# Placing the products of the spectral pairs further behind their elementwise pieces in a fused Fourier-mixer, ELU feed-forward and top-1 expert kernel

## Chip, cores and metric

The kernel runs on one core of a Trainium2 chip. The metric is the device time of one execution in microseconds (us), the median over runs.

## What is computed

Eight sequences of 3072 tokens with 256 channels pass through three layers:

```
X = rfft(x, axis=1);  Xr, Xi = X.real, X.imag
Yr = Xr @ w_r - Xi @ w_i + b_r
Yi = Xr @ w_i + Xi @ w_r + b_i
Y* = sign(Y*) * max(|Y*| - 0.01, 0)          # soft threshold, both parts
y  = irfft(Yr + 1j*Yi, n=3072)
h  = y @ w_in;  g = where(h > 0, h, exp(min(h, 0)) - 1)
z  = g @ w_out                               # feed-forward, d_ff 2048
# top-1 of 8 experts by normalised logits: out = gate * (relu(z @ w1[e]) @ w2[e])
```

Every product is done in three half-precision matmuls (high x high, high x low, low x high), so every operand is first split into a high half and a low half; these splits are the elementwise pieces named below.

## The kernel before

The program is a fixed order of instructions written out by hand: each engine runs its own list in order, and waits where an operand is not there. There are four stages. The first does the spectral layer of sequence 0. Then come eight batches, one for each sequence. A batch is 128 steps: 8 blocks of 384 tokens by 16 slices of the feed-forward layer. A step issues `ffn1` (six matmuls of 384 columns into a PSUM tile of `ps_h`, line 527, then exponential and relu on ScalarE, lines 539 and 540, and the maximum on VectorE, line 543) and `ffn2` of a slice four steps back (nine matmuls of 264 columns into `ps_a`, line 553). Every second step also splits two slices, high half on ScalarE (line 98, `copy_hi`) and low half on VectorE (line 101, `copy_lo`), into `ghl`. The last stage is the expert layer.

While batch b runs its feed-forward, the spectral layer of sequence b + 1 is threaded between the steps; the eighth batch has none. A list `plan` of (position in steps, function) says where. An entry at 53.3 is issued in step 53 between `ffn1` and `ffn2`, one at 53.6 after `ffn2`. Its parts, for each sequence:

- 16 `unit_a` (line 181, first transform), each after a `split_x` of its input; SyncE writes the results to DRAM (`b_d`, line 192), and `load_b` (line 200) reads them back as `b_in`, in another layout.
- 12 `pair`s, each of two groups of frequencies: a generator that `OFF` cuts into 17 pieces, placed at offsets from the pair's start. Starts run evenly from `PA` to `PZ`. Pieces 0 and 1 are the first product (line 222, from `b_in` into tile ps0) with the high split and a copy on ScalarE (lines 98, 234); 2 to 5 are elementwise on VectorE, VectorE, ScalarE, VectorE (lines 101, 242, 98, 101: `s_t`, `sm`); 6 is the first mixing product (line 210, from the `s_t` made of `sm`, with `k` on ScalarE, line 261, and `u` on GpSimd, line 262); 7 and 8 are the other mixing products; 9 to 12 are the threshold on VectorE (lines 276, 281, 290: `mt`, `mc`, `my`); 13 splits the high half `mm` on ScalarE (line 297), 14 the low half (line 299); 15 is the inverse product (line 304), with the high split of `do`; 16 its low split and the write to `e_d` (line 316).
- `unit_e` (line 329), two for each block, reads `e_d` back through `load_e` (line 204) and makes the next feed-forward input `yT`.

`ps_h` has four PSUM buffers, taken in turn: `ffn1`, `unit_a`, `unit_e`, the routing product (line 629) and the four products of a pair (pieces 0, 6, 7, 15) all draw from this ring in the stages after the first, so a tile must have been read by ScalarE and VectorE before the fourth product after it. The splitting of expert weights (GpSimd, lines 504 to 506) and its DMAs (`wl`, line 476 or 479; `wexp_d`, line 507) are issued at fixed steps, and so stand in SyncE's list between the others.

Of the kernel before, what the change touches and what calls it, by code (L numbers as in the profile page):

```python
# [15 lines left out]
ALU = mybir.AluOpType  # L16
# [3 lines left out]
B, S, D = 8, 3072, 256  # L20
# [19 lines left out]
XP = 2  # L40
JC = 4
CG, CN, CV = 4, 12, 8
PA, PZ = 44.0, 108.0
OFF = (0, 0.5, 1.0, 1.5, 2.0, 2.5, 3.5, 5.0, 5.5, 6.0, 6.5, 7.0, 7.5, 8.3, 8.8, 10.2, 11.0)
NP = NJ // 2
CD = (1, 2, 3, 5, 6, 7)
LAM = float(np.float32(0.01))
# [7 lines left out]
def kernel(  # L55
# [22 lines left out]
    act, dve, pool, pe, sp = nc.scalar, nc.vector, nc.gpsimd, nc.tensor, nc.sync  # L78
# [18 lines left out]
    def copy_hi(o, i, k):  # L97
        act.activation(out=o, in_=i, func=AF.Copy, scale=k)  # L98

    def copy_lo(o, i, k, hi):  # L100
        dve.scalar_tensor_tensor(out=o, in0=i, scalar=k, in1=hi, op0=ALU.mult, op1=ALU.subtract)  # L101
# [56 lines left out]
    def load_x(b, i):  # L158
        src = x[b].rearrange("(n m) c -> n m c", m=N2)[:, 4 * i : 4 * i + 4, :]
        if b == 0:  # L160
            if i == 0:
                xpc[0] = pre.tile([96, N2, D], F32, name="x_0")
            t = xpc[0][:, 4 * i : 4 * i + 4, :]
        else:
            t = xp.tile([N1, 4, D], F32, tag="xpc", name="xpc")
        sp.dma_start(out=t, in_=src)
        xpc[b, i] = t

    def split_x(b, g):
        src = xpc[b, g // 2][:, 2 * (g % 2) : 2 * (g % 2) + 2, :]  # L170
        t = xs.tile([N1, 2, 2, D], F16, tag="xsp", name="xsp")
        copy_hi(t[:, 0], src, 2.0**9)
        copy_lo(t[:, 1], src, 2.0**9, t[:, 0])
        xsp[b, g] = t
# [22 lines left out]
    def load_b(b, c):  # L197
        if c < NJ // JC:
            b_in[b, c] = bc.tile([128, JC, 2 * D], F16, tag="b_in", name="b_in")
            sp.dma_start(out=b_in[b, c], in_=b_d[b % 2][:, c * JC : (c + 1) * JC, :])  # L200

    def load_e(b, blk):
        e_in[b, blk] = ec.tile([96, 4, 2 * D], F16, tag="e_in", name="e_in")
        sp.dma_start(out=e_in[b, blk], in_=e_d[b % 2][:, 4 * blk : 4 * blk + 4, :])
# [10 lines left out]
    def pair(b, p):  # L215
# [27 lines left out]
        if p == 0:  # L243
# [3 lines left out]
                out=s2z[:, 0, :, 0:1], in0=z[:, :, 1:2], scalar1=2.0**-12, scalar2=None, op0=ALU.mult  # L247
# [11 lines left out]
        k = mx.tile([128, D], F32, tag="k1", name="k1")  # L259
# [3 lines left out]
            out=u, in0=bias[:, 0 if p else 1], in1=k[:, None, :].to_broadcast([128, 2, D]), op=ALU.add  # L263
# [6 lines left out]
        if p == 0:  # L270
# [3 lines left out]
        c = mx.tile([128, 2, D], F32, tag="mc", name="mc")  # L274
        y = mx.tile([128, 2, D], F32, tag="my", name="my", bufs=2)
        dve.scalar_tensor_tensor(
            out=t, in0=ps2.rearrange("p (r d) -> p r d", r=2), scalar=2.0**-10, in1=u, op0=ALU.mult, op1=ALU.add
# [7 lines left out]
        for jj in range(2):  # L285
            for r in range(2):
                i = slice(64 * jj, 64 * jj + 64)
# [3 lines left out]
                else:  # L291
                    dve.scalar_tensor_tensor(
                        out=o, in0=c[i, r, :], scalar=-1.0, in1=t[i, r, :], op0=ALU.mult, op1=ALU.max
                    )
            yield
        m = mx.tile([128, 2, 2, D], F16, tag="mm", name="mm", bufs=2)
        act.activation(out=m[:, 0], in_=y, func=AF.Copy)  # L297
        yield
        pool.tensor_tensor(out=m[:, 1], in0=y, in1=m[:, 0], op=ALU.subtract)  # L299
        yield  # L300
        ps3 = spec_ps()
        for jj in range(2):
# [14 lines left out]
            out=e_d[b % 2][8 * p : 8 * p + 8].rearrange("(j q) m x -> (q m) j x", j=2),  # L317
# [21 lines left out]
    def step_a(b, i):  # L339
        def one():  # L340
            if i + 2 < 16:
                split_x(b, i + 2)

        def two():
            if b and i % 2 == 1 and (i - 1) // 2 + XP < 8:
                load_x(b, (i - 1) // 2 + XP)
            unit_a(b, i)

        return one, two

    def units_e(b, blk):
        return [lambda cc=cc: unit_e(b, blk, cc) for cc in range(2)]
# [168 lines left out]
    def ffn1(b, blk, f, prev):  # L521
        y = yT[b, blk]
        ps = ps_h.tile([128, 512], F32, tag="h", name="ps_h")
        n = 0
        for cc in range(2):
            for i, h in ((0, 0), (0, 1), (1, 0)):
                pe.matmul(  # L527
                    ps[:, 0:BLK],
                    lhsT=win[:, i, cc, f * 128 : (f + 1) * 128],
                    rhs=y[:, h, cc, :],  # L530
                    start=n == 0,
                    stop=n == 5,
                )
                n += 1
        if f % 2 == 0:
            h_t[b, blk, f // 2] = tp.tile([128, 2, BLK], F32, tag="g", name="g")
        g = h_t[b, blk, f // 2][:, f % 2]
        e = tp.tile([128, BLK], F32, tag="e", name="e")
        act.activation(out=e, in_=ps[:, 0:BLK], func=AF.Exp, scale=2.0**-19)  # L539
        act.activation(out=e, in_=e, func=AF.Relu, scale=-(2.0**19), bias=top)  # L540
        if prev:
            split_hi(prev)
        dve.scalar_tensor_tensor(out=g, in0=e, scalar=-1.0, in1=ps[:, 0:BLK], op0=ALU.mult, op1=ALU.max)  # L543
        if prev:
            split_lo(prev)
# [125 lines left out]
    with tc.tile_pool(name="pre", bufs=1, side="right") as pre:  # L671
        for k in range(8):
# [5 lines left out]
                out=wm[ri].rearrange("p (k c) -> p k c", k=2), in_=w.rearrange("(k p) c -> p k c", p=128)  # L678
# [7 lines left out]
        for src, parts in (  # L686
# [3 lines left out]
            for lo, hi, v, r in parts:  # L690
                first.append(
                    lambda src=src, lo=lo, hi=hi, v=v, r=r: pool.dma_start(
                        out=bias[lo:hi, v, r, :], in_=src.partition_broadcast(hi - lo)
# [44 lines left out]
        for i in range(NP + 2):  # L738
# [3 lines left out]
            if i == 0:  # L742
                dve.tensor_scalar(
                    out=bias, in0=bias, scalar1=16.0, scalar2=-LAM * 16.0, op0=ALU.mult, op1=ALU.add
# [301 lines left out]
    NS = NBLK * NF  # L1046
    for b in range(B):
        plan = []
        for blk in range(1, NBLK):
            at = (2, 4, 9, 20, 30, 40, 50)[blk - 1] if b + 1 == B else 16 * blk - 11  # L1050
            if blk > 1:
                plan.append((max(0, at - 6), lambda blk=blk: load_e(b, blk)))
            for n, u in enumerate(units_e(b, blk)):
                plan.append((at + 1.5 * n, u))
        if b + 1 < B:
            plan.append((0, lambda: [load_x(b + 1, k) for k in range(XP)]))
            for i in range(2):
                plan.append((2.5 + i, lambda i=i: split_x(b + 1, i)))
            for i in range(16):
                for m, fn in enumerate(step_a(b + 1, i)):  # L1060
                    plan.append((3.4 + 2.25 * i + 0.6 * m, fn))
            for c in range(3):
                plan.append((41.2, lambda c=c: load_b(b + 1, c)))
            for k in range(NP):
                p = PA + (PZ - PA) * k / (NP - 1)
                gen = pair(b + 1, k)
                for o in OFF:
                    plan.append((p + o, lambda gen=gen: next(gen)))
                if k % 2 == 1 and k > 1:
                    plan.append((p + 0.2, lambda k=k: load_b(b + 1, k // 2 + 2)))  # L1070
            for blk in range(2):
                plan.append((NS - 6.2, lambda blk=blk: load_e(b + 1, blk)))
            for n, u in enumerate(units_e(b + 1, 0)):
                plan.append((NS - 2.6 + n, u))
        plan.sort(key=lambda p: p[0])
        if b + 1 == B:
            plan.append((60, open_moe))
        for blk in range(NBLK):
            for f in range(NF):
                step = blk * NF + f  # L1080
                ffn1(b, blk, f, pend.pop(0) if pend and f % 2 == 0 else None)
                if f % 2:
                    pend.append((b, blk, f // 2))
                while plan and plan[0][0] < step + 0.5:
                    plan.pop(0)[1]()
                run_late(1 + (len(late) > 1))
                todo.append((b, blk, f))
                lag = LAG + 1 if todo[0][2] == 0 or f == LAG + 1 else LAG
                while len(todo) > lag:
                    pop_ffn2()  # L1090
                while plan and plan[0][0] < step + 1:
                    plan.pop(0)[1]()
                run_late(1 + (len(late) > 1))
                c = b * NBLK + blk
                if f in wexp_at.get(c, ()):
                    if nw[0] + 1 < 8 * NE:
                        wexp_load(nw[0] + 1)
                    wexp_split(nw[0])
                    nw[0] += 1
        for _, u in plan:  # L1100
            u()
    while pend:
        k = pend.pop(0)
# [9 lines left out]
    for i in range(len(seq) + 1):  # L1113
# [12 lines left out]
        for h in range(2):  # L1126
            if 0 <= i - h < len(seq):
                kind, k = seq[i - h]
# [110 lines left out]
```

## Time and profile before

| what | value |
|---|---|
| median of 3 runs | 4063.5 us (4059.53 to 4069.39) |
| the profiled execution | 4070.74 us, of which span 4069.0 us |
| TensorE (PE) matmuls busy | 3719.3 us, 91% |
| VectorE (DVE) busy | 2586.8 us, 64% |
| ScalarE (ACT) busy | 2344.9 us, 58% |
| GpSimd (POOL) busy | 1428.6 us, 35% |
| mean granted TensorE clock | 0.967 of full speed |

The busy times are of one profiled execution on the chip, and times in the views count from the first instruction. A row names the line of the kernel, the engine, the operation and the tiles as out<-in. Idle time of an engine is put down to whatever ended it last. PEld is the loading of weights on TensorE, which overlaps matmuls. Because the matmuls are pipelined, the start of the next instruction tells the pace better than the duration of one.

### The profile page before, as it was taken

The page shows a single profiled execution, that of the slowest core. Times are in us where ns is not written, and L with a number is a line of the kernel's source. Part 1 is how long each engine was busy: PE and PEld are TensorE (multiplying, and loading weights), DVE is VectorE, ACT ScalarE, POOL GpSimd, SP SyncE. Part 2 cuts the span into 40 slices and gives each one's busy share as a digit, 9 for nine tenths or more (in the row PEclk, how much of TensorE's full clock was granted, in tenths as well). Part 3 has the DMA queues.
Part 4 walks back from the last instruction along what each step waited for, and adds up shares of the span by engine and source line. Part 5 has one row for each costly group of instructions (what it writes and reads, how often), then busy time and mean ns, then how long its engine had stood idle before and what let it go on. Part 6 is the DMA issues. An engine that isn't in the chain of part 4 may idle for free. (4 is left out here: it accounts for less than half of the span.)

```text
span 4069.0 us, 80617 instructions
## 1 busy us (share of the span) xinstructions
PE 3719.3 (91%) x31580; PEld 2909.5 (72%) x31580; DVE 2586.8 (64%) x5366; ACT 2344.9 (58%) x4738; POOL 1428.6 (35%) x1669
## 2 busy tenths in 40 slices
PE   5798898889889998988998898899999999999998
PEld 3566666667666666766666676667787899999998
DVE  7766676767666676766666776766565555555554
ACT  4676686668667666866776686667752222222221
POOL 3223323333333333333233323333234444344443
PEclk7899999999999999999999999999999999999999
DMA  6331132113112221211221131111035355534332
GB/s 191 99 85 49 45 97 61 54 48 106 46 46 79 73 62 48 88 53 56 63 86 51 44 99 60 54 53 56 20 101 128 78 154 152 147 79 113 95 82 78
DMA packets 290223, 323.25 MB, mean 79 GB/s; under 512 B 172197, under 2 KB 239023, under 8 KB 281520
## 3 DMA queue, kind: packets, MB, share of 16 engines
q1 hardware_dynamic: 238688, 197.12, 18.7%
q0 software_dynamic: 51152, 120.97, 8.9%
q8 instruction: 247, 4.05, 0.4%
q14 instruction: 136, 1.11, 0.1%
HBM read 335.96 MB, written 120.36 MB: 112 GB/s over the span
## 5 line engine op out<-in xcount | busy, mean ns | idle before, releaser
L553 PE MATMUL ps_a<-wout,ghl 128*128 128x264 f16 x9216 | 1229.9, 281 | 4.6 <-DVE ghl L101 3.7
L527 PE MATMUL ps_h<-yT,win 128*128 128x384 f16 x6144 | 1180.3, 330 | 15.9 <-DVE g L543 9.5
L543 DVE SCALAR_TENSOR_TENSOR g<-e,ps_h 128x384 f32<-128x384 f32 x1024 | 564.4, 551 | 802.4 <-ACT e L540 799.6
L553 PEld LDWEIGHTS <-ghl 128*128 128x128 f16 x9216 | 906.8, 100 | 223.0 <-DVE ghl L101 5.3
L527 PEld LDWEIGHTS <-win 128*128 128x128 f16 x6144 | 602.5, 99 | 340.3 <-issue 36.8
L539 ACT ACTIVATE e<-ps_h 128x384 f32<-128x384 f32 x1024 | 494.5, 483 | 440.6 <-PE ps_h L527 421.9
L968 ACT ACTIVATE r<-ps_h 128x512 f32<-128x512 f32 (+1 forms) x440 | 244.7, 556 | 803.9 <-PE ps_h L962 780.2
L540 ACT ACTIVATE e<-e,top 128x384 f32<-128x384 f32 x1024 | 629.9, 615 | 33.2
L962 PE MATMUL ps_h<-xt,wbuf 128*128 128x256 f16 (+1 forms) x5280 | 557.1, 263 | 6.5 <-DMA wbuf<-wexp_d,wix_f 6.5
L101 DVE SCALAR_TENSOR_TENSOR ghl<-g,ghl 128x768 f16<-128x768 f32 x512 | 506.3, 989 | 82.5 <-ACT ghl L98 79.4
L983 PE MATMUL ps_a<-wbuf,g 128*128 128x256 f16 x4776 | 554.6, 273 | 2.1 <-DVE g L970 1.1
L962 PEld LDWEIGHTS <-wbuf 128*128 128x128 f16 x5280 | 478.5, 98 | 56.9 <-DMA wbuf<-wexp_d,wix_f 6.8
L983 PEld LDWEIGHTS <-g 128*128 128x128 f16 x4776 | 465.0, 98 | 56.8 <-DVE g L970 2.2
L98 ACT ACTIVATE ghl<-g 128x768 f16<-128x768 f32 x512 | 423.4, 827 | 0.6 <-DVE g L543 0.6
L210 PE MATMUL ps_h<-wmix,s_t 128*128 128x256 f16 x1590 | 242.9, 284 | 178.7 <-DVE s_t L101 150.0
L1001 POOL DMA_INDIRECT out_dram<-o,mt x199 | 207.9, 1044 | 524.1 <-DVE o L993 301.3
L648 POOL DMA_INDIRECT rows_d<-row,pi x192 | 205.5, 1070 | 512.1 <-DMA rows_d<-row,pi 210.1
L969 DVE CAST g<-r 128x512 f16<-128x512 f32 (+1 forms) x440 | 177.6, 404 | 285.0 <-ACT r L968 282.6
L210 PEld LDWEIGHTS <-s_t 128*128 128x128 f16 x1728 | 164.2, 102 | 259.1 <-DVE s_t L101 182.8
L970 DVE TENSOR_TENSOR g<-r,g 128x512 f16<-128x512 f32 (+1 forms) x440 | 282.7, 643 | 15.1
L299 POOL TENSOR_TENSOR mm<-my,mm 128x512 f16<-128x512 f32 x96 | 125.3, 1305 | 462.3 <-ACT mm L297 461.8
L593 POOL TENSOR_TENSOR row<-xf,row 128x256 f16<-128x256 f32 x192 | 157.0, 818 | 297.5 <-ACT row L592 296.9
(191 smaller groups left out, 3547.5 us busy)
## 6 DMA issues: line engine op xcount, KB each, us to landing
b_d<-ao SPq DMA_DIRECT2D x128, 192.0 KB, 2.2
b_in<-b_d SPq DMA_DIRECT2D x48, 512.0 KB, 5.8
e_d<-do SPq DMA_DIRECT2D x96, 256.0 KB, 2.2
e_in<-e_d SPq DMA_DIRECT2D x64, 384.0 KB, 5.8
xpc<-in_x_dram SPq DMA_DIRECT2D x56, 384.0 KB, 4.1
wl<-in_moe_w_dram SPq DMA_DIRECT2D x64, 256.0 KB, 3.1
wexp_d<-wh SPq DMA_DIRECT2D x64, 256.0 KB, 3.5
raw<-in_moe_w_out_dram SPq DMA_DIRECT2D x8, 512.0 KB, 7.9
```

Of the source, the lines that this page charges most:

```text
L98: act.activation(out=o, in_=i, func=AF.Copy, scale=k)
L101: dve.scalar_tensor_tensor(out=o, in0=i, scalar=k, in1=hi, op0=ALU.mult, op1=ALU.subtract)
L210: pe.matmul(o, lhsT=st(h, cc), rhs=wmix[:, w, i, cc, :], start=first and n == 0, stop=last and n == 5)
L527: pe.matmul(ps[:, 0:BLK], lhsT=win[:, i, cc, f * 128 : (f + 1) * 128], rhs=y[:, h, cc, :], start=n == 0, stop=n == 5,)
L539: act.activation(out=e, in_=ps[:, 0:BLK], func=AF.Exp, scale=2.0**-19)
L540: act.activation(out=e, in_=e, func=AF.Relu, scale=-(2.0**19), bias=top)
L543: dve.scalar_tensor_tensor(out=g, in0=e, scalar=-1.0, in1=ps[:, 0:BLK], op0=ALU.mult, op1=ALU.max)
L553: pe.matmul(a_t[b, blk][t][:, 0:WOC], lhsT=g[:, h, f % 2, t * 128 : (t + 1) * 128], rhs=wout[:, f, i, :], start=f == 0 and n == 0, stop=f ...
L962: pe.matmul(ps[:, j, 0:n], lhsT=w[:, c : c + 128], rhs=xt[:, 2 * h + cc, :], start=m == 0, stop=m == 5)
L968: act.activation(out=r[:, :, 0:n], in_=ps[:, :, 0:n], func=AF.Relu, scale=2.0**-9)
L970: dve.tensor_tensor(out=g[:, q, 1, :, 0:n], in0=r[:, :, 0:n], in1=g[:, q, 0, :, 0:n], op=ALU.subtract)
L983: pe.matmul(ps[:, 0:D], lhsT=g[:, f // 2, h, f % 2, t * 128 : (t + 1) * 128], rhs=w[:, c : c + 256], start=m == 0, stop=m == 23,)
```

## The change

The offsets between pieces become longer. The first mixing product (piece 6) moves from 3.5 to 4.8 steps, so from 1.0 to 2.3 steps behind the last piece it reads (piece 5, at 2.5); the other mixing products from 5.0 and 5.5 to 7.0 and 7.5; the threshold follows; the inverse product (piece 15) moves from 10.2 to 14.2, so from 1.4 to 3.7 steps behind the low split of `mm`. Pairs start at 41.0 to 102.8 in place of 44.0 to 108.0, one every 5.62 steps in place of 5.82. The low split of `mm` goes from GpSimd to VectorE in all but the first sequence. The first transforms stand 2.1 steps apart in place of 2.25, the first two loads of x for a sequence are issued 8 steps before the end of the batch ahead, and the loads of `b_in` are placed at 38.8 in place of 41.2.

```diff
-PA, PZ = 44.0, 108.0
-OFF = (0, 0.5, 1.0, 1.5, 2.0, 2.5, 3.5, 5.0, 5.5, 6.0, 6.5, 7.0, 7.5, 8.3, 8.8, 10.2, 11.0)
+PA, PZ = 41.0, 102.8
+OFF = (0, 0.5, 1.0, 1.5, 2.0, 2.5, 4.8, 7.0, 7.5, 8.0, 8.5, 9.0, 9.5, 10.0, 10.5, 14.2, 15.2)
...
-        pool.tensor_tensor(out=m[:, 1], in0=y, in1=m[:, 0], op=ALU.subtract)
+        (dve if b else pool).tensor_tensor(out=m[:, 1], in0=y, in1=m[:, 0], op=ALU.subtract)
...
-            plan.append((0, lambda: [load_x(b + 1, k) for k in range(XP)]))
+            if b == 0:
+                plan.append((0, lambda: [load_x(b + 1, k) for k in range(XP)]))
+            if b + 2 < B:
+                plan.append((NS - 8, lambda: [load_x(b + 2, k) for k in range(XP)]))
             for i in range(2):
-                plan.append((2.5 + i, lambda i=i: split_x(b + 1, i)))
+                plan.append((2.5 + i if b == 0 else 0.5 + 1.2 * i, lambda i=i: split_x(b + 1, i)))
             for i in range(16):
                 for m, fn in enumerate(step_a(b + 1, i)):
-                    plan.append((3.4 + 2.25 * i + 0.6 * m, fn))
+                    plan.append((4.4 + 2.1 * i + 0.6 * m, fn))
             for c in range(3):
-                plan.append((41.2, lambda c=c: load_b(b + 1, c)))
+                plan.append((38.8, lambda c=c: load_b(b + 1, c)))
```

VectorE's list for the third pair of the sequence handled in the fourth batch (`s_t<-ps_h` is piece 2, `sm` piece 3, `s_t<-sm` piece 5, `my` pieces 11 and 12 of the pair before), first as it was:

```order
L101 SCALAR_TENSOR_TENSOR s_t<-ps_h,s_t 128x2x256
L290 TENSOR_TENSOR my<-mt,mc 64x256 x2
L604 TENSOR_REDUCE mxv<-lg 128x3
L543 SCALAR_TENSOR_TENSOR g<-e,ps_h 128x384
L242 TENSOR_TENSOR sm<-ps_h,sm 128x256
L290 TENSOR_TENSOR my<-mt,mc 64x256 x2
L606 TENSOR_TENSOR lg<-lg,mxv 128x24
L608 SCALAR_TENSOR_TENSOR eq<-lg,wdec 128x24
L543 SCALAR_TENSOR_TENSOR g<-e,ps_h 128x384
L101 SCALAR_TENSOR_TENSOR ghl<-g,ghl 128x768
L101 SCALAR_TENSOR_TENSOR s_t<-sm,s_t 128x2x128
```

And the same pair as it is now:

```order
L101 SCALAR_TENSOR_TENSOR s_t<-ps_h,s_t 128x2x256
L242 TENSOR_TENSOR sm<-ps_h,sm 128x256
L543 SCALAR_TENSOR_TENSOR g<-e,ps_h 128x384
L101 SCALAR_TENSOR_TENSOR ghl<-g,ghl 128x768
L101 SCALAR_TENSOR_TENSOR yT<-ps_h,yT 128x384
L276 SCALAR_TENSOR_TENSOR mt<-ps_h,u 128x512
L101 SCALAR_TENSOR_TENSOR s_t<-sm,s_t 128x2x128
```

The four `my` instructions of the pair before no longer stand between the pieces that the first mixing product waits for; one `mt` does. A little later in the same list stands the instruction that came from GpSimd (line 299):

```order
L543 SCALAR_TENSOR_TENSOR g<-e,ps_h 128x384
L101 SCALAR_TENSOR_TENSOR ghl<-g,ghl 128x768
L290 TENSOR_TENSOR my<-mt,mc 64x256 x2
L101 SCALAR_TENSOR_TENSOR do<-ps_h,do 128x2x256
L602 TENSOR_TENSOR lg<-xf,ss 128x24
L604 TENSOR_REDUCE mxv<-lg 128x3
L543 SCALAR_TENSOR_TENSOR g<-e,ps_h 128x384
L299 TENSOR_TENSOR mm<-my,mm 128x512
```

Four instructions stand between it and the last `my` that it reads. SyncE's list in the fourth batch around the first loads of `b_in`, as it was:

```order
L204 DMA e_in<-e_d 96x2048
L192 DMA b_d<-ao 96x2x512 x4
L476 DMA wl<-in_moe_w_dram 128x512
L507 DMA wexp_d<-wh 128x2x512
L200 DMA b_in<-b_d 128x2048 x3
L204 DMA e_in<-e_d 96x2048
```

And now:

```order
L204 DMA e_in<-e_d 96x2048
L192 DMA b_d<-ao 96x2x512 x3
L200 DMA b_in<-b_d 128x2048 x3
L476 DMA wl<-in_moe_w_dram 128x512
L507 DMA wexp_d<-wh 128x2x512
L204 DMA e_in<-e_d 96x2048
```

The three loads stood behind the write of `wexp_d`, which waits for GpSimd; they now stand right behind the last write of `b_d`.

## Rows read from the trace of the kernel before

**Rows 1.** Busy time by stage: seven batches with spectral work, the eighth batch, the experts.
```profile
core 0: us, PE busy (x) PEld busy (x) DVE busy (x) ACT busy (x) POOL busy (x), PEclk, DMA share, GB/s
...
172.00:2727.00 2555.00, 2307.67 (x18650) 1702.71 (x18648) 1722.22 (x3560) 1801.50 (x3685) 835.95 (x1045) 0.97 0.22 64
2727.00:2999.00 272.00, 265.94 (x2169) 196.63 (x2167) 167.72 (x383) 210.58 (x423) 93.57 (x138) 1.00 0.22 64
2999.00:4069.00 1070.00, 1050.52 (x10096) 944.76 (x10093) 568.55 (x1164) 248.17 (x452) 447.05 (x432) 0.99 0.41 107
```

**Rows 2.** Waits of PE from 172 to 2727 us: us in total, times, longest.
```profile
PE ps_h L210 <- DVE s_t L101: 145.3, 70, 4.8
PE ps_h L304 <- POOL mm L299: 30.5, 14, 3.2
PE ps_h L210 <- ACT s_t L98: 19.1, 35, 0.9
PE ps_h L222 <- DMA b_in<-b_d: 11.7, 6, 2.7
PE ps_h L304 <- ACT mm L297: 9.4, 7, 1.3
PE ps_h L527 <- DVE g L543: 9.0, 14, 0.8
PE ps_h L329 <- DVE do L101: 4.9, 7, 0.7
PE ps_h L527 <- DVE do L101: 4.7, 7, 0.7
PE ps_h L210 <- DVE g L543: 4.6, 7, 0.7
```

**Rows 3.** Timeline of PE, fourth batch, second and third pair: start, length, count, idle before.
```profile
1391.47 0.39 PE L210 MATMUL ps_h<-wmix,s_t 128*128 128x256 f16 x2 [0.93 <-ACT s_t L98]
1394.99 1.03 PE L210 MATMUL ps_h<-wmix,s_t 128*128 128x256 f16 x4 [3.12 <-DVE s_t L101]
...
1409.51 1.14 PE L527 MATMUL ps_h<-yT,win 128*128 128x384 f16 x6
...
1411.50 1.14 PE L527 MATMUL ps_h<-yT,win 128*128 128x384 f16 x6
...
1419.69 1.03 PE L210 MATMUL ps_h<-wmix,s_t 128*128 128x256 f16 x4 [4.77 <-DVE s_t L101]
```

**Rows 4.** Timeline of DVE ahead of the last of these waits.
```profile
1412.18 0.84 DVE L290 TENSOR_TENSOR my<-mt,mc 64x256 f32<-64x256 f32 x2
...
1413.60 0.42 DVE L242 TENSOR_TENSOR sm<-ps_h,sm 128x256 f32<-128x256 f32 x1
...
1418.26 1.37 DVE L101 SCALAR_TENSOR_TENSOR s_t<-sm,s_t 128x256 f16<-128x256 f32 x1
```

**Rows 5.** Timeline of POOL at the same time.
```profile
1417.95 1.41 POOL L299 TENSOR_TENSOR mm<-my,mm 128x512 f16<-128x512 f32 x1 [10.09 <-ACT mm L297]
```

**Rows 6.** Tile s_t in the fourth batch: ns min/median/max.
```profile
L101 DVE SCALAR_TENSOR_TENSOR s_t<-sm,s_t x12: 412/418/1376, 1376.4 to 1585.7; 128x256 f16<-128x256 f32 x12
```

**Rows 7.** Tile g of the experts, 3200 to 3300 us: ns min/median/max.
```profile
L970 DVE TENSOR_TENSOR g<-r,g x43: 424/693/694, 3200.0 to 3300.0; 128x512 f16<-128x512 f32 x36, 128x256 f16<-128x256 f32 x7
```

**Rows 8.** Busy time in the fourth batch: stretch of first transforms, stretch of pairs (columns of rows 1).
```profile
1264.00:1366.00 102.00, 101.29 (x797) 73.45 (x795) 75.80 (x153) 86.93 (x180) 33.48 (x48) 1.00 0.31 91
1366.00:1610.00 244.00, 210.21 (x1712) 156.25 (x1710) 159.16 (x335) 157.32 (x325) 84.34 (x102) 0.95 0.15 49
```

**Rows 9.** Timeline of SP's DMA issues, fourth batch, before the first pair.
```profile
1340.55 15.28 SPq L192 DMA_DIRECT2D b_d<-ao  x4
...
1363.59 0.38 SPq L507 DMA_DIRECT2D wexp_d<-wh  x1
1364.14 1.93 SPq L200 DMA_DIRECT2D b_in<-b_d  x3
```

**Rows 10.** Timeline of PE: last first transform, first product of the first pair.
```profile
1352.31 0.81 PE L181 MATMUL ps_h<-xsp,f_sb 96*96 96x512 f16 x3
...
1368.78 0.51 PE L222 MATMUL ps_h<-t_sb,b_in 128*128 128x128 f16 x6 [1.23 <-DMA b_in<-b_d]
```

## The prediction

> **What bounds the kernel now.** I read the busy times by stage first. In the seven batches that carry spectral work, TensorE is busy 2307.7 of 2555 us at 0.97 of its full clock; in the eighth batch, which has the same feed-forward work and no pairs, it is busy 265.9 of 272 us at full clock [rows 1]. So TensorE sets the pace, and what it loses lies in the seven batches: 2555 - 2307.7 = 247.3 us idle, and 3% of 2555 = 77 us from granted clock at the lower of its two levels (1.2 for 2.4 GHz). Within one batch the loss is local. The stretch of first transforms loses 0.7 us and keeps the clock at 1.00; the stretch of pairs loses 244 - 210.2 = 33.8 us and has a clock of 0.95, so another 12 us [rows 8].
>
> The waits say for what [rows 2]. The first mixing product waits for `s_t`: 145.3 us for VectorE's half and 19.1 us for ScalarE's, 164.4 in all, about 2 us for each of 84 pairs. The inverse product waits 30.5 + 9.4 = 39.9 us for `mm`. The first product of a sequence waits 11.7 us for `b_in`. A third kind is waits of a product for a `ps_h` buffer that VectorE has not yet read: 9.0 + 4.9 + 4.7 + 4.6 = 23.2 us. The rest is under a us each or little more.
>
> Idle time and clock together are 324 us. The profiled execution took 4070.7 us, 7.2 us above the median of the runs. With none of the 324 us left it would take 3747 us. (Some us of the idle time fell in stretches at the low clock and stand in both terms, so this floor is rather low than high.)
>
> **The change part by part.**
>
> *First mixing product.* A plain step takes 1411.50 - 1409.51 = 1.99 us [rows 3], for 6 x 384 + 9 x 264 = 4680 columns, so six matmuls of 256 columns take 1.99 x 1536/4680 = 0.65 us. Piece 6 moves 1.3 steps further from the last piece that it reads: 2.6 us. For most pairs the inverse product of the pair two before (at 14.2 - 11.2 = 3.0 steps) now stands in that gap too: 3.2 us of cover. The average wait of 2 us is under this. The two large ones of a batch are not: the second pair waits 0.93 + 3.12 = 4.05 us and has no inverse product in its gap, so 4.05 - 2.6 = 1.45 remain; the third waits 4.77 us, so 1.57 remain [rows 3]. That is 3.0 us for each batch, 21 us for seven, of 164. Bounds: nothing remains, since the four `my` that stood in VectorE's list between `sm` and its predecessor are gone from there, and two of them took 0.84 us ahead of `sm` [rows 4]; or twice as much, 40 us, if routing work meets more pairs than these two at the new spacing. I take 21.
>
> *Inverse product.* 2.3 steps or 4.6 us of further distance, against a longest wait of 3.2 us [rows 2]: all 39.9 us go.
>
> *Low split on VectorE.* It adds an instruction of 512 elements in each of 84 pairs. VectorE's subtraction of the same shapes and types in the expert stage takes 693 ns [rows 7], so 8.3 us for each batch. The product that reads it stands 3.7 steps or 7.4 us behind, and it replaces an instruction of GpSimd that took twice as long (1.41 us [rows 5]). Queued behind it are VectorE's `g` and `ghl` of the next step, so the cost, if its cover is gone, is 0.69 us each time, 58 us in all. There is also a gain: VectorE's `s_t<-sm` took 1.37 us where its median is 0.42 [rows 4, 6], and it ended 0.27 us after the GpSimd split that ran beside it [rows 5]. Without that split such delays become rarer. I cost it at nothing, with 0 and 58 us as ends; the range keeps both.
>
> *Loads of b_in.* The last first transform starts at 1352.31, its write to `b_d` has been issued by 1355.8, and the loads are issued only at 1364.14, right behind the write of `wexp_d`; the product starts at 1368.78, 4.6 us after, and had waited 1.23 us [rows 9, 10]. Now nothing stands between the last write and the loads. If a write lands about as late as a load, 4.6 us, the data are there at the latest 9.2 us after the issue, so 12.7 us after the start of the transform. TensorE reached the product at 1368.78 - 1.23, which is 15.2 us after the transform; the distance shrinks by two steps (37.75 to 44 becomes 36.5 to 41, counted by the places that steps offer), so to 11.3 us. A write is a small transfer and should land well before 4.6 us, so I take 0 of the 11.7 us as left; the upper end is 1.4 us for each batch, 10 us.
>
> *The ring of ps_h.* This is what is late next. The products of the pairs are now spread (offsets 0, 4.8, 1.4 and 3.0 within a spacing of 5.62, where they stood at 0, 3.5, 5.0 and 4.4 within 5.82), which favours it. But TensorE no longer pauses, so ScalarE and VectorE no longer catch up in the pauses. In the stretch of pairs VectorE is busy 159.2 + 8.3 = 167.5 us and ScalarE 157.3, against 210 - 12 = 198 us of TensorE at full clock: 85% and 79% [rows 8]. ScalarE ran at 86.9/102 = 85% in the stretch of first transforms, and TensorE lost 0.7 us there [rows 8]; a share of 85% alone does not stop it. I take the ring's 23 us times 1.5: 35 us, with 10 and 70 as ends. The closer first transforms (2.1 steps) are in this term.
>
> *Clock.* At both stretches where TensorE idles little the clock is 1.00 [rows 1, 8]. With the waits of 4 us gone I take 10 of 77 us as left; ends 0 and 25.
>
> *Loads of x.* Two loads move from the start of a batch to eight steps before it, onto SyncE's list, and nothing on TensorE waited for x in rows 2. No cost, and no gain.
>
> Sum: 3747 + 21 + 35 + 10 = 3813 us against 4070.7, and 7 less against the median: **3806 us**.
>
> **The rivals.**
>
> *Half comes back.* The elementwise chain itself may be too slow: ScalarE waits for VectorE and VectorE for ScalarE within a pair, and at 85% in-order lists leave little room, so the waits move to the feed-forward's own `ps_h` and `ghl`. For it: the busy shares above. Against it: rows 2 show at most 0.8 us for each ring wait. Half of 324 back is 3747 + 162 - 7 = 3902 us. Chance 0.12.
>
> *VectorE blocked by GpSimd.* The 1.37 us beside the GpSimd split [rows 4, 5] show that VectorE can lose 1.37 - 0.42 = 0.95 us to one GpSimd instruction. The moved split also reads two tiles in SBUF, and GpSimd keeps its other work. If each of the 84 were blocked so and TensorE waited each time, 80 us come on top: 3886 us. Chance 0.07, because 7.4 us of cover stand behind the split.
> The Trainium skill (Perfetto Trace Analysis, Optimizing Scalar/DVE Operations) speaks for this rival: the two engines share a read port, so that offloading work between them might not help; SBUF — State Buffer (two separate sides) calls it a lock held for a whole instruction. The 1.37 us agree with a lock; whether the moved split meets it no row of before can show.
>
> *Slower: the ring stops TensorE.* Four buffers serve 77 feed-forward tiles and 48 pair tiles in the stretch of pairs. If every pair product waited for VectorE to read the tile four places before it, 48 waits for each batch would use up the 324/7 = 46 us at 0.96 us each. At 1.2 us each: 3747 + 7 x 48 x 1.2 - 7 = 4143 us. Today's waits are up to 0.8 us and hit few products [rows 2]. Chance 0.03.
>
> *No change.* If in-order lists made every piece late by as much as the products moved, each wait would stay: 4063 us. The `my` that left the list, one group of which stood ahead of `sm` [rows 4], speak against it. Chance 0.02.
>
> **How the numbers follow.** Forecast 0.73, from 3752 to 3878 us: low with nothing of the mixing waits and clock left and 10 us of the ring (3750), high with 40 + 70 + 25 us (3875). Better than that: 0.03. The forecast's range takes in neither the half that comes back (0.12) nor slower (0.03) nor no change (0.02); of the blocked VectorE (0.07) it holds the lower part. So about 0.2 lie outside, and this is the range. Faster by over 0.2% (about what a measurement tells from no change): 0.95; within: 0.02; slower: 0.03.
>
> **What would show it.** In the profile after, each step shows as follows. PE's wait for `s_t` on VectorE falls from 145 to some 20 us over the seven batches; waits for `mm` and `b_in` are gone; line 299 stands on VectorE 84 times at about 0.7 us; the ring's waits for `g` and `do` are the largest left, 20 to 70 us; the clock of the seven batches is 0.99 or more; these take 2290 to 2310 us in place of 2555; the eighth batch and the experts take what they took. The prediction is wrong if PE's idle time in the seven batches stays above 130 us, or if VectorE's idle time goes to nothing there, or if `s_t` still leads the waits.

## The result, and the profile after

The changed kernel takes 3888.97 us (3888.15 to 3892.49) against 4064.19 us for the kernel before, run beside it. The ratio is 0.957 (95% interval 0.9554 to 0.9587), so 175 us or 4.3% faster. I had forecast 3806 us and a range of 3752 to 3878. The direction was right, the gain was two thirds of what I expected, and the time lies 11 us above the range. The profiled execution after took 3889.22 us.

First the stages, cut as in [rows 1] (same columns: PE, PEld, DVE, ACT, POOL busy, granted clock, DMA share, GB/s):

```profile
172.00:2547.00 2375.00, 2250.87 (x18644) 1688.21 (x18643) 1795.16 (x3644) 1782.79 (x3685) 743.86 (x961) 0.99 0.23 69
2547.00:2826.00 279.00, 269.43 (x2173) 197.95 (x2171) 167.81 (x384) 210.67 (x424) 91.41 (x138) 0.99 0.21 63
2826.00:3887.00 1061.00, 1048.49 (x10094) 943.82 (x10091) 568.47 (x1163) 247.98 (x452) 446.46 (x432) 1.00 0.41 108
```

The seven batches with spectral work went from 2555 to 2375 us, which is the whole gain. TensorE's idle time there fell from 247.3 to 2375 - 2250.9 = 124.1 us, and the clock rose from 0.97 to 0.99. The floor below both is the same within the rounding of the clock to a hundredth (some 12 us either way): 2555 - 247 - 77 = 2231 us by the sum of the prediction, 2375 - 124 - 24 = 2227 us now. The eighth batch lost 7 us and the experts won 9; 6.5 us of the latter are the experts' first wait for their weights (`wbuf`), which is gone.

TensorE's waits in the seven batches, answering to [rows 2] (who waited for whom: us in total, times, longest):

```profile
PE ps_h L527 <- DVE g L543: 44.6, 36, 2.5
PE ps_h L527 <- DVE do L101: 28.6, 28, 1.4
PE ps_h L222 <- DVE g L543: 12.7, 7, 1.8
PE ps_h L210 <- DVE g L543: 10.7, 26, 0.5
PE ps_h L222 <- DVE do L101: 9.6, 7, 1.4
PE ps_a L553 <- DVE ghl L101: 5.0, 14, 0.6
PE ps_h L629 <- DVE g L543: 4.9, 7, 0.7
PE ps_h L629 <- DVE mt L276: 2.5, 7, 0.4
```

No wait for `s_t`, `mm` or `b_in` is left, which were 164, 40 and 12 us. But a kind of wait that was 23 us before is now 114 us (the lines of `ps_h` that name `g`, `do` or `mt`): a product that does not need the data named waits until VectorE has read the tile four places back in the ring.

ScalarE's own waits in the seven batches show a second difference. Before:

```profile
ACT s_t L98 <- DVE sm L242: 92.3, 63, 2.3
ACT lg L611 <- DVE eq L608: 59.1, 48, 1.9
...
ACT mm L297 <- DVE my L290: 28.7, 42, 1.8
```

After:

```profile
ACT mm L297 <- DVE my L290: 123.7, 77, 2.1
ACT lg L611 <- DVE eq L608: 111.1, 55, 3.7
ACT s_t L98 <- DVE sm L242: 52.1, 49, 1.6
```

ScalarE waits longer at two places. The high split of `mm` (piece 13) now stands half a step behind the last piece of the threshold (piece 12), where it stood 0.8 of a step behind, and ScalarE waits there 124 us in place of 29. The routing's `lg`, for VectorE's `eq`, waits 111 us in place of 59; no experiment below undoes that one. What stands behind such a wait in ScalarE's list is, among others, the exponential of the feed-forward. One place of the first kind in the fourth batch, ScalarE, then VectorE, then TensorE (start, length, idle before):

```profile
1312.36 0.63 ACT L297 ACTIVATE mm<-my 128x512 f16<-128x512 f32 x1 [1.40 <-DVE my L290]
...
1313.83 0.49 ACT L539 ACTIVATE e<-ps_h 128x384 f32<-128x384 f32 x1
...
1317.05 0.48 ACT L539 ACTIVATE e<-ps_h 128x384 f32<-128x384 f32 x1
1317.56 0.61 ACT L540 ACTIVATE e<-e,top 128x384 f32<-128x384 f32 x1
```

```profile
1313.51 2.01 DVE L299 TENSOR_TENSOR mm<-my,mm 128x512 f16<-128x512 f32 x1
...
1318.21 0.55 DVE L543 SCALAR_TENSOR_TENSOR g<-e,ps_h 128x384 f32<-128x384 f32 x1 [1.36 <-ACT e L540]
```

```profile
1318.82 1.14 PE L527 MATMUL ps_h<-yT,win 128*128 128x384 f16 x6 [1.97 <-DVE g L543]
```

ScalarE lost 1.40 us at `mm` and shows no idle time from there until after the second `e`, so what it lost there reached that tile: its `g` ended at 1318.76, and the next `ffn1` had waited 1.97 us for that buffer.

The low split on VectorE took 2.01 us here. Over the seven batches (ns min/median/max):

```profile
L299 DVE TENSOR_TENSOR mm<-my,mm x84: 677/1557/2015, 293.7 to 2519.6; 128x512 f16<-128x512 f32 x84
```

My row for it was 693 ns [rows 7]. It meets GpSimd's `u`, whose `k` is made of piece 6 at 4.8 steps while the split stands at 10.5 - 5.62 = 4.9 steps of the next pair:

```profile
1313.68 1.27 POOL L262 TENSOR_TENSOR u<-bias,k 128x512 f32<-128x512 f32 x1
```

The `u` ended at 1314.95, the split 0.57 us later. In turn VectorE's `s_t<-sm`, which had taken up to 1376 ns beside the split on GpSimd [rows 6], is clean now:

```profile
L101 DVE SCALAR_TENSOR_TENSOR s_t<-sm,s_t x84: 411/416/560, 274.2 to 2497.8; 128x256 f16<-128x256 f32 x84
```

Three accounts of the 114 us were open: theory R, that the ring of four is too short for tiles held so long; theory A, that ScalarE's wait for `my` makes the readers late; and theory D, that VectorE has too much to do (with the held-up split as its worst part).

### The profile page after: what moved, and what is told of

The parts are those of the page before. It is cut to its first block, busy times and chain, and to the rows that moved or that the text cites. A ratio compares the mean times of both kernels' runs of the same rounds, so it can differ in the third digit from the quotient of the medians.

```text
span 3887.4 us, 80595 instructions
## 1 busy us (share of the span) xinstructions
PE 3663.1 (94%) x31580; PEld 2894.5 (74%) x31580; DVE 2660.1 (68%) x5450; ACT 2326.3 (60%) x4738; POOL 1333.7 (34%) x1585
## 5 line engine op out<-in xcount | busy, mean ns | idle before, releaser
L553 PE MATMUL ps_a<-wout,ghl 128*128 128x264 f16 x9216 | 1209.1, 277 | 13.1 <-DVE ghl L101 11.9
L553 PEld LDWEIGHTS <-ghl 128*128 128x128 f16 x9216 | 893.7, 98 | 224.4 <-DVE ghl L101 21.1
L262 POOL TENSOR_TENSOR u<-bias,k 128x512 f32<-128x512 f32 x96 | 130.4, 1358 | 606.9 <-ACT k L261 606.7
L970 DVE TENSOR_TENSOR g<-r,g 128x512 f16<-128x512 f32 (+1 forms) x440 | 282.5, 642 | 15.1
L210 PE MATMUL ps_h<-wmix,s_t 128*128 128x256 f16 x1590 | 225.4, 280 | 18.6 <-DVE g L543 10.7
L593 POOL TENSOR_TENSOR row<-xf,row 128x256 f16<-128x256 f32 x192 | 168.8, 879 | 187.6 <-ACT row L592 186.5
L210 PEld LDWEIGHTS <-s_t 128*128 128x128 f16 x1728 | 172.7, 101 | 75.7 <-issue 17.8
```

What stands on the lines that cost most here:

```text
L210: pe.matmul(o, lhsT=st(h, cc), rhs=wmix[:, w, i, cc, :], start=first and n == 0, stop=last and n == 5)
L553: pe.matmul(a_t[b, blk][t][:, 0:WOC], lhsT=g[:, h, f % 2, t * 128 : (t + 1) * 128], rhs=wout[:, f, i, :], start=f == 0 and n == 0, stop=f ...
L970: dve.tensor_tensor(out=g[:, q, 1, :, 0:n], in0=r[:, :, 0:n], in1=g[:, q, 0, :, 0:n], op=ALU.subtract)
```

## The experiments

Each kernel is the changed one with the edit shown, unless it says otherwise, and each was run beside the kernel before. Differences from the changed kernel are taken between the ratios to before, of 4064 us.

**One step later for the splits of mm.**

```diff
-OFF = (..., 9.5, 10.0, 10.5, 14.2, 15.2)
+OFF = (..., 9.5, 11.0, 11.5, 14.2, 15.2)
```

> The changed kernel (3889.0 us, 17.7 us of PE idle a batch, nearly all of it waits for a ps_h buffer that VectorE has not read) with pieces 13 and 14 (the splits of mm) one step later, at 11.0 and 11.5. In the changed kernel ScalarE waits 17.8 us for my in one batch's stretch of pairs, where it waited 4.1 us before, because piece 13 now stands half a step behind piece 12. Theory A (ScalarE held up behind my makes the feed-forward's exponentials, and so the reading of ps_h, late): ScalarE's wait for my falls to about 4 us a batch, PE's waits for ps_h by 5 us a batch, so about 3855 us. Theory R (the ring is held by the pairs' own tiles) and theory D (VectorE has too much work): within 10 us of 3889.

Measured: 3846.95 us, ratio 0.9466 (0.945 to 0.9482), so 42 us faster. TensorE's idle time fell from 17.7 to 13.8 us a batch, 28 us in all, and the mean granted clock of the execution rose from 0.980 to 0.983. ScalarE's wait for `my` over seven batches, and the largest of TensorE's ring waits:

```profile
ACT mm L297 <- DVE my L290: 14.9, 14, 1.7
PE ps_h L527 <- DVE g L543: 37.8, 22, 3.7
```

This is what theory A says, but not it alone: the split on VectorE was free of `u` as well, with a median of 684 ns. It is also not the whole: the ring's waits that were 114 us are still 85 in the same places.

**The last split of the pair sooner.**

```diff
-OFF = (..., 14.2, 15.2)
+OFF = (..., 14.2, 14.7)
```

> The changed kernel with piece 16 (low split of do, which is the last reader of the inverse product's ps_h tile) half a step sooner, at 14.7. PE's waits that end with that piece are 39.2 us over the seven batches. Theory R (the pairs' own tiles hold the ring too long): these fall to about 10 us and the time to about 3860 us. Theories A and D: the tile is freed sooner but VectorE's list is as full, so the waits move to g, and the time stays within 10 us of 3889.

Measured: 3885.51 us, ratio 0.9555 (0.9535 to 0.9574): no difference from the changed kernel that can be measured. The tile was freed sooner, and the waits moved on:

```profile
PE ps_h L527 <- DVE g L543: 49.7, 43, 3.1
PE ps_h L222 <- DVE g L543: 20.0, 21, 2.2
PE ps_h L527 <- DVE do L101: 15.3, 14, 1.6
```

Behind `do` there were 38 us and are now 17; behind `g` they rose from 57 to 70 in these places. This is not a clean test of theory R, though. The next pair's pieces 11 and 12, which make `my`, stand at 9.0 + 5.62 = 14.6 and 9.5 + 5.62 = 15.1 steps. At 15.2 piece 16 stood behind both, at 14.7 it stands between them. VectorE's list in one such place, and ScalarE's wait for `my`, which was 123.7 us:

```profile
1339.76 0.84 DVE L290 TENSOR_TENSOR my<-mt,mc 64x256 f32<-64x256 f32 x2
1340.64 0.69 DVE L101 SCALAR_TENSOR_TENSOR do<-ps_h,do 128x512 f16<-128x512 f32 x1
1341.36 0.86 DVE L290 TENSOR_TENSOR my<-mt,mc 64x256 f32<-64x256 f32 x2
```

```profile
ACT mm L297 <- DVE my L290: 155.7, 77, 2.7
```

So what the ring gained by `do`, ScalarE may have lost again behind `my`; no run parts the two.

**Five buffers in the ring.**

```diff
-    ps_h = ctx.enter_context(tc.tile_pool(name="ps_h", bufs=4, space=PSUM))
-    ps_a = ctx.enter_context(tc.tile_pool(name="ps_a", bufs=4, space=PSUM))
+    ps_h = ctx.enter_context(tc.tile_pool(name="ps_h", bufs=5, space=PSUM))
+    ps_a = ctx.enter_context(tc.tile_pool(name="ps_a", bufs=3, space=PSUM))
```

> The changed kernel with five ps_h buffers and three ps_a buffers. Theory R and theory A (all of the loss is the ring of four, whatever makes the readers late): PE's waits for ps_h fall from 120 to about 40 us over the seven batches; the accumulators then wait for their evacuation, up to 0.8 us for each of 64 blocks, so 3810 to 3860 us. Theory D (VectorE cannot keep up, so the waits only show at the ring): the waits move to ghl, and the time stays within 15 us of 3889 or rises by the accumulators' waits.

Measured: 3805.02 us, ratio 0.9362 (0.9347 to 0.9378), so 84 us faster. TensorE's waits in the seven batches:

```profile
PE ps_a L553 <- DVE ghl L101: 21.4, 49, 0.6
PE ps_h L527 <- DVE do L101: 16.9, 14, 1.6
PE ps_h L222 <- DVE do L101: 14.4, 14, 1.2
PE ps_h L527 <- DVE g L543: 6.0, 14, 0.5
PE ps_a L553 <- ACT ghl L98: 4.5, 14, 0.4
PE ps_h L329 <- DMA e_in<-e_d: 1.1, 4, 0.4
```

The waits for `ps_h` fell from 114 to 37 us, and no wait of the accumulators for their evacuation is listed, with three buffers in place of four; the time is 5 us below the range that allowed for such waits. `ghl` came up from 5 to 26 us (28 in the texts on record below, whose stretch took in some of the eighth batch): the feed-forward's own chain is the next one in line. VectorE has as much to do as before, so theory D does not hold in its plain form; the 84 us were the ring's. Theories R and A both expected this, so it does not part them.

**The low split back on GpSimd.**

```diff
-        (dve if b else pool).tensor_tensor(out=m[:, 1], in0=y, in1=m[:, 0], op=ALU.subtract)
+        pool.tensor_tensor(out=m[:, 1], in0=y, in1=m[:, 0], op=ALU.subtract)
```

> The changed kernel with the low split of mm on GpSimd again. Theory D: VectorE has 8.3 us less a batch and the ring waits fall, 3830 to 3870 us. The prediction's costing (nothing, with cover of 3.7 steps) and theories A and R: within 10 us of 3889. The rival of the lock from the other side (GpSimd's split holds up VectorE's short pieces by 0.95 us at a time): 3900 to 3950 us.

Measured: 3886.71 us, ratio 0.956 (0.9544 to 0.9576): no difference. The part of the change that moves this instruction gives nothing and costs nothing, although on VectorE it takes 1557 ns. ScalarE's wait for `my` was 123.9 us here too.

**The low split alone one step later**, to part theory A from the held-up split:

```diff
-OFF = (..., 10.0, 10.5, 14.2, 15.2)
+OFF = (..., 10.0, 11.5, 14.2, 15.2)
```

> The changed kernel with piece 14 alone one step later, at 11.5, piece 13 left at 10.0. Moving both gave 3847 us; that also took the low split out of the way of GpSimd's u (on VectorE the split fell from a median of 1557 ns to 684 ns). Theory A (it was ScalarE's wait for my, which piece 13 sets): the split falls to about 690 ns here too, ScalarE still waits over 100 us for my, and the time stays within 12 us of 3889. The lock (it was the split held up by GpSimd): 3847 us, give or take 10.

Measured: 3890.19 us, ratio 0.9551 (0.9536 to 0.9567): no difference. The rows:

```profile
L299 DVE TENSOR_TENSOR mm<-my,mm x84: 674/684/1160, 299.0 to 2517.1; 128x512 f16<-128x512 f32 x84
ACT mm L297 <- DVE my L290: 123.6, 77, 2.1
```

The split is at its own price again and ScalarE's wait is unchanged, and so is the time. This kernel and that of the first experiment differ in piece 13 alone: 0.9551 against 0.9466, or 35 us. The gain of the first experiment therefore came with piece 13 on ScalarE, not with the split's own duration.

**The first mixing product back near its data.**

```diff
-OFF = (0, 0.5, 1.0, 1.5, 2.0, 2.5, 4.8, 7.0, ...)
+OFF = (0, 0.5, 1.0, 1.5, 2.0, 2.5, 3.5, 7.0, ...)
```

> The changed kernel (3889.0 us) with piece 6, the first mixing product, back at 3.5, one step behind piece 5. The prediction's step (the distance of 1.3 steps is what removed the wait for s_t, 164 us over seven batches before): the wait for s_t comes back with 100 to 165 us, part of it in place of ring waits, so 3960 to 4030 us. The rival (the my that left VectorE's list ahead of sm did it, and the distance was not needed): s_t waits stay under 40 us and the time within 30 us of 3889.

Measured: 3907.07 us, ratio 0.9617 (0.9601 to 0.9633), so 19 us slower. The wait for `s_t` came back with a fifth of its 164 us:

```profile
PE ps_h L210 <- DVE s_t L101: 33.0, 42, 1.7
PE ps_h L210 <- DVE g L543: 27.0, 42, 1.5
```

My expectation failed and the rival held: without the `my` of the pair before in its way, `s_t` is nearly in time at one step of distance.

**The my around sm again, near and far.** Pieces 11 to 16 at 12.2, 12.7, 13.8, 14.3, 16.2 and 17.2, so that two `my` stand on either side of piece 2 in VectorE's list and all four ahead of `sm` (before the change two of them stood behind `sm`), with the first mixing product at 3.5 in one kernel and at 4.8 in the other.

```diff
-OFF = (..., 4.8, 7.0, 7.5, 8.0, 8.5, 9.0, 9.5, 10.0, 10.5, 14.2, 15.2)
+OFF = (..., 3.5, 7.0, 7.5, 8.0, 8.5, 12.2, 12.7, 13.8, 14.3, 16.2, 17.2)
```

> The changed kernel with piece 6 at 3.5 and pieces 11 to 16 at 12.2, 12.7, 13.8, 14.3, 16.2 and 17.2: the first mixing product is one step behind its data again, and the four my of the pair before stand around sm in VectorE's list again, as before the change. If those my are what made s_t late: PE's waits for s_t, 33 us over seven batches with piece 6 at 3.5 alone, come back to 110 to 170 us. If the distance alone mattered: they stay at 25 to 50 us. The time itself moves with the other pieces too, and is not the measure here.

> As the kernel with the my around sm, but piece 6 at 4.8. The prediction's working (1.3 steps of distance cover the average wait and leave 3 us a batch): PE's waits for s_t are 10 to 40 us over seven batches. If s_t is late by more than that with the my in its way: over 60 us.

Measured: 3959.69 us near (ratio 0.9726, 0.971 to 0.9742) and 3845.68 us far (0.9442, 0.9426 to 0.9458). Near, the largest wait of TensorE is once more

```profile
PE ps_h L210 <- DVE s_t L101: 108.3, 77, 3.3
```

which with 3.3 us for ScalarE's half is the low end of what the first account expected. Far there is none, less than either account of that kernel expected; the list begins with

```profile
PE ps_h L304 <- DVE g L543: 27.6, 21, 1.9
PE ps_h L527 <- DVE g L543: 26.6, 35, 1.3
PE ps_h L329 <- DMA e_in<-e_d: 11.9, 7, 2.1
```

So either half of the change would have removed the wait for `s_t`: the distance alone, with the `my` in the way, or nearly so the order alone. The far kernel is also 52 us faster than the changed one: there piece 13 stands 1.1 steps behind piece 12, and no wait of ScalarE for `my` appears among its largest. Several pieces moved in it, so the 52 us are not put down to one of them.

**The inverse product back near its data.**

```diff
-OFF = (..., 10.5, 14.2, 15.2)
+OFF = (..., 10.5, 11.9, 12.9)
```

> The changed kernel with pieces 15 and 16, the inverse product and the last split, at 11.9 and 12.9, so 1.4 steps behind the low split of mm as before the change. The prediction's step: the waits for mm come back with about 40 us, 3915 to 3945 us. Rival (the split is made in time at 1.4 steps, and the piece's new place among the ring's products is what counts): no wait for mm, and the time moves by the ring alone, 3870 to 3905 us.

Measured: 3965.88 us, ratio 0.9763 (0.9747 to 0.978), so 78 us slower: more than I expected.

```profile
PE ps_h L304 <- DVE mm L299: 82.9, 53, 2.4
PE ps_h L527 <- DVE g L543: 40.8, 27, 4.2
```

The waits for `mm` are 83 us, twice those of before. The split now stands in VectorE's full list and took 1580 ns at the median; which of the two makes it late was not separated. Of the parts undone here it is the one that costs most.

**Five buffers in the kernel before.** Only the two pool lines of the third experiment, applied to the kernel before.

> The kernel before with five ps_h buffers and three ps_a buffers, nothing else changed. If the ring bound the kernel before only by its 27 us of waits while the products waited for their data: 4035 to 4070 us. If the ring was behind the waits for s_t as well (late exponentials because of late buffers): under 4000 us.

Measured: 4029.18 us, ratio 0.9921 (0.9904 to 0.9937), so 32 us faster, a little more than the ring's waits there: 6 us below the first range and far from the second. The waits for data stay:

```profile
PE ps_h L210 <- DVE s_t L101: 154.8, 77, 4.8
PE ps_h L304 <- POOL mm L299: 30.0, 14, 2.6
```

The ring was not behind them. The fifth buffer is worth 32 us before the change and 84 after it.

**Edits together.** Five buffers with pieces 13 and 14 at 11.0 and 11.5:

> Five ps_h buffers with pieces 13 and 14 at 11.0 and 11.5, piece 16 left at 15.2. Five buffers alone gave 3805 us, all three edits 3765 us. If ScalarE's wait for my still costs time with five buffers (it makes ghl late, 28 us of PE's waits there): 3775 to 3788 us, with the waits for ghl under 15 us and those behind piece 16 still near 31 us. If the ring of five hides it and piece 16 was the rest: 3800 to 3810 us.

Measured: 3786.15 us, ratio 0.9307 (0.9291 to 0.9322); the waits for `ghl` fell to 5 us and those behind piece 16 from 31 to 23. With piece 16 at 14.7 as well:

> Five ps_h buffers, pieces 13 and 14 at 11.0 and 11.5, and piece 16 at 14.7 together. With five buffers alone 3805 us, 9.3 us of PE idle a batch, of it 31 us over seven batches behind piece 16 and 28 us behind ghl. If the causes add up (ScalarE's wait for my makes ghl late, piece 16 holds the ring): idle falls to 3 to 5 us a batch, 3765 to 3785 us. If the ring of five already hides what the later mm gives: 3795 to 3805 us.

Measured: 3764.92 us, ratio 0.9271 (0.9255 to 0.9286). This version beats both kernels, by 7.3% and by 3.1%. TensorE idles 2249 - 2220.65 = 28 us in its seven batches, at full clock:

```profile
172.00:2421.00 2249.00, 2220.65 (x18666) 1677.80 (x18665) 1760.02 (x3644) 1774.79 (x3685) 748.64 (x961) 1.00 0.24 73
```

Piece 16, which gave nothing that can be measured with four buffers, gives 15 us here (0.9307 to 0.9271). Two things differ, the fifth buffer and pieces 13 and 14 a step later, and no run tells which of them it needed. ScalarE still waits 117 us for `eq` in this version, so with five buffers that wait costs little.

The loads of `b_in` and of x, the closer first transforms and the new spacing of the pairs were not undone by themselves.

## Why the prediction was right and wrong

*What bounds the kernel, and the floor.* Right. Idle time and clock of the seven batches were all that could be won: 2231 us by the prediction, 2227 us from the profile after, and 2221 us of TensorE in the best version.

*First mixing product.* I left 21 of 164 us; none was left. The distance covered every pair, the two large ones included. I treated the order on VectorE as a bound on the good side only. The experiments show that it would have done most of it by itself (33 us of `s_t` waits with it, 108 us without, both at one step).

*Inverse product.* All 40 us gone, as said; undoing it costs 78.

*Low split on VectorE.* Costed at nothing, and it was nothing (3886.71 against 3888.97 us), though the price of the instruction was wrong: 1557 ns for 693. Nor did it replace one that took twice as long: I had taken 1.41 us from one row, and GpSimd's median over the seven batches was 1256 ns. The rival in which GpSimd holds it up was right about the mechanism and wrong about the path, since the product stands 3.7 steps behind it. The Trainium skill (SBUF — State Buffer, two separate sides) says that a VectorE operation with two inputs in SBUF and a GpSimd operation that reads SBUF shut each other out of a shared port for a whole instruction. The rows agree: the split took 684 ns at the median out of `u`'s way and 1557 ns where most of the 84 met it. The Trainium skill (Perfetto Trace Analysis, Optimizing Scalar/DVE Operations) also says that moving work between the two might not help, because they share that port. The time did not move, but not for this reason: it did not move either when the split was out of `u`'s way (3890.19 us).

*Loads of b_in.* None of the 11.7 us left, as said. No experiment moved the loads back, so that their place did it is read from the order and the missing wait alone. The eighth batch and the experts did not take quite what they took; the parts, 7 us more and 9 us less, nearly cancel.

*The ring of ps_h.* This is the step that failed. "I take the ring's 23 us times 1.5: 35 us, with 10 and 70 as ends": it was 114 us. I named the mechanism, that TensorE no longer pauses and so the readers no longer catch up, but sized it by a factor without a row behind it, and I read the even spread of the products as a relief. That the loss is the ring's is shown by the fifth buffer, which takes its waits to 37 us and gives 84 us back. What I did not see is that the same table of offsets put piece 13 half a step behind piece 12, so that ScalarE stood still for VectorE 124 us, with the exponentials that free the ring behind it. Undoing that gives 35 us back against the kernel with the low split later, 42 against the changed one, which the intervals do not tell apart. Some 85 us of ring waits remain then, and which reader is late there is open: the lost pauses are one account, which fits a fifth buffer that is worth 32 us before the change and 84 after it; ScalarE's longer wait for `eq` (still 105 us in that kernel) is another. Neither was tested by itself with four buffers. The closer first transforms, which I had put into this term, are not it: in the fourth batch TensorE loses 0.2 of 95 us in their stretch and 16.8 of 225 us in that of the pairs. I took ScalarE's busy share (79%, and 85% elsewhere without harm) as the measure; an in-order engine that waits is not busy, so the share could not show it.

*Clock.* 10 us left by the prediction, 1% of 2375 = 24 us by the profile, with 124 us of TensorE idle; with five buffers, where it idles 2290 - 2224.9 = 65 us, the clock of the seven batches was 1.00.

The sum then reads: 3813 us, less 21 for the mixing waits, plus 79 for the ring, 14 for the clock and 5 for `ghl`, is 3890 us, against 3889.2 for the profiled execution; that it meets it so closely is partly luck, since the clock's term is rounded by 12 us.

Of the rivals, *VectorE blocked by GpSimd* gave 3886 us and was nearest in number, by luck: its 80 us were to be waits of TensorE for the blocked split, and there are none. *Half comes back*, at 3902 us, was nearer in mechanism: the waits did move to the feed-forward's own `ps_h`, and ScalarE did wait for VectorE within a pair. Its reason, too full engines, is not what the runs show: taking the split off VectorE changed nothing, and piece 13 a step later or a fifth buffer gave part of the time back with the work the same.

Of my signs of being wrong none appeared: TensorE's idle time, 124 us, stayed just under the 130 us that I had named. That bound was looser than the upper end of the range, which holds 40 + 70 = 110 us of waits.

## What to carry to other kernels

When waits for data are removed from the engine that sets the pace, the readers behind it may lose the pauses in which they caught up, so do not size the next wait (here a ring of PSUM tiles taken in turn) from its waits of today; how long each tile is held is the better start, though no run here tries such a sizing. After a list of offsets is changed, look at every pair of neighbouring pieces on two engines, also those whose result is not urgent: a piece that waits stops everything behind it on its engine. Look also at what a moved piece now stands in front of: the last split half a step sooner took 21 us off the waits behind it and, standing between the two halves of `my` on VectorE, put 32 us on ScalarE's wait for them.

## What was not expected of the hardware

A two-input subtraction on VectorE took 684 ns at the median out of the way of a GpSimd addition and 1557 ns where most of its 84 runs met one, and the meeting with the GpSimd split had cost a short VectorE split up to 0.96 us before; in the changed kernel the time did not depend on it. Three accumulator buffers in PSUM for three accumulators in use were enough: waits for their evacuation came to 2.9 us over seven batches in the kernel before with five ring buffers, and to none that is listed in the changed kernel with five.
